# Spectrum rows of an S4 convolution kernel: real and imaginary parts interleaved over the partitions, in place of one half of the partitions each

## The chip, the cores and the metric

The kernel runs on one core of one Trainium2 chip. The metric is the device time of one execution in microseconds (us); the time of the kernel before is the median of three runs. The profile comes from one more execution, with a trace of every engine: PE (TensorE), DVE (VectorE), ACT (ScalarE), POOL (GpSimd) and SP (SyncE, whose queue issues most transfers).

## What is computed

Four residual layers over x of 2048 positions by 512 channels: attention over a dilated window (A), a state-space convolution (B), A again, B again, with a layer norm in front of each.

```python
x = x + A(layernorm(x));  x = x + B(layernorm(x))
x = x + A(layernorm(x));  x = x + B(layernorm(x))

# B: a convolution along the sequence, one kernel K per channel
P  = exp(logdA[:, :, None] * l)
K  = einsum("dn,dnl,dn->dl", Cc, P, dB).real
Kf = rfft(pad(K));  Uf = rfft(pad(u))
y  = irfft(Uf * Kf)[:L] + u * Dskip
```

Both B layers have the same parameters, so the spectrum Kf of the convolution kernel is the same in both.

## The kernel before, in words

`k_gen` makes K in the first 150 us or so, while `build_b_consts` makes the tables of the transform (F1, w2, Wp, WpJ, g2) and layer A's projections run beside it. Then comes A's core, then B (class `FftB`), then A and B again. A's core shifts its values along the partitions by transfers from `v_ext` to itself, partitions 0 to 111 to 1 to 112 in one of them (L305, around 439 us in the second A layer).

B's transform has two steps each way. The 512 channels are cut into 2 groups g (`NG`) of 64 columns of 4 channels (`DQG`). `f1` is the first forward step: 8 tiles per group, each of 16 matmuls (L523) into one PSUM tile `pb`, copied out to `a1s` (L512). `f2` is the second: 8 chunks `ec` of 16 frequencies, each of 16 matmuls against the table `w2_sb` (L532). The rows of its product, which are the 128 partitions, are 64 real rows and 64 imaginary rows of the spectrum: `w2` is built so that rows 0 to 63 are real and rows 64 to 127 imaginary. `i1` and `i2` are the two inverse steps; `i1` contracts over those 128 rows with the tables Wp and WpJ (L574, L575).

The spectrum of K goes through memory, since both B layers use it. `k_f2` copies each chunk from PSUM into a tile `kf_sb` (L512, three buffers) and stores it to `kf_dram[g, ec]`, whose layout is 64 rows of (real, imaginary), by two transfers: partitions 0 to 63 to the real places, 64 to 127 to the imaginary ones (L541, 128 KB each). `u_f2` needs each row of the spectrum of K, real and imaginary, on both partitions that hold this row of u's spectrum. So per chunk two transfers load all 64 rows of 4 KB, once into partitions 0 to 63 and once into 64 to 127 of a slot of `kf_ring` (L556, 256 KB each; 4 slots). ACT copies u's chunk to `ub` (L558, three buffers), and two multiplications on DVE (L559 by the real, L560 by the imaginary part) give `t1` and `t2`, from which `i1` goes on.

The generators are interleaved by `zip_run`: `f1` of group 1 beside `k_f2` of group 0, `f1` of u beside `k_f2` of group 1, `f1` of u's group 1 beside `u_f2` of group 0, then `u_f2` of group 1 beside `i1` of group 0. Copies out of PSUM alternate between ACT and DVE (`evac`), `pb` has four buffers. In the first B layer (time 280 to 357) both the stores and the loads of the spectrum run; `kf_ring` lies there in the memory of `k_perm`, so its first load has to wait for the last matmul that reads `k_perm` (L523 of `f1` of group 1). In the second B layer (540 to 575) only the loads run, and the first four slots are filled some 40 us ahead, in layer A. A scheduler of the build sets the order of instructions on each engine; each engine and the SP queue take theirs in that order.

Of the kernel before, what the change touches and what calls it, by code (L numbers as in the profile page):

```python
# [10 lines left out]
ACT = mybir.ActivationFunctionType  # L11
ALU = mybir.AluOpType
# [3 lines left out]
BF16 = mybir.dt.bfloat16  # L16
I32 = mybir.dt.int32

P = 128
# [345 lines left out]
def build_b_consts(nc, cpool, tmp, w2_dram, g2_dram):  # L365
    C = {}
    pi_i = tmp.tile([P, 1], I32, name="p_i")
# [4 lines left out]
    t_i = tmp.tile([P, 8], I32, name="pk_t")  # L372
    nc.vector.tensor_scalar(t_i[:, 0:1], pi_i[:], 63, 2, ALU.bitwise_and, ALU.logical_shift_right)
    nc.vector.tensor_scalar(t_i[:, 1:2], pi_i[:], 6, None, ALU.logical_shift_right)
    nc.vector.tensor_scalar(t_i[:, 2:3], pi_i[:], 3, None, ALU.bitwise_and)
    nc.vector.tensor_scalar(t_i[:, 3:4], pi_i[:], 15, None, ALU.bitwise_and)
    nc.vector.tensor_scalar(t_i[:, 4:5], pi_i[:], 6, None, ALU.logical_shift_right)
    nc.vector.tensor_scalar(t_i[:, 5:6], pi_i[:], 4, 3, ALU.logical_shift_right, ALU.bitwise_and)
    nc.vector.tensor_scalar(t_i[:, 6:7], pi_i[:], 63, 1, ALU.bitwise_and, ALU.logical_shift_left)
    nc.vector.tensor_copy(t_i[:, 7:8], pi_i[:])  # L380
    pk = tmp.tile([P, 8], F32, name="pk"); nc.vector.tensor_copy(pk[:], t_i[:])
    ak, rik, d4k, cm, rim, d4m = (pk[:, j:j + 1] for j in range(6))
# [5 lines left out]
    dmask_k = tmp.tile([P, 4], F32, name="dmask_k")  # L388
# [4 lines left out]
    def off_cols(name, rcol, v00, v10, v01, v11):  # L393
        o = tmp.tile([P, 2], F32, name=name)
        nc.vector.tensor_scalar(o[:, 0:1], rcol, float(v10 - v00), float(v00), ALU.mult, ALU.add)
        nc.vector.tensor_scalar(o[:, 1:2], rcol, float(v11 - v01), float(v01), ALU.mult, ALU.add)
        return o
# [9 lines left out]
    off = off_cols("w2_off", rik, 2048, 0, 4096, 2048)  # L407
    s8 = 2.0 * math.pi / 8192 * SIN_SHRINK
    ECH = 16
    for ch in range(P // ECH):  # L410
        es = slice(ch * ECH, (ch + 1) * ECH)
        base = tmp.tile([P, ECH, 16], I32, name="w2_base")
        nc.gpsimd.iota(base[:], pattern=[[2, ECH], [512, 16]], base=1 + 2 * ch * ECH, channel_multiplier=0)
        qi = tmp.tile([P, ECH, 2, 16], I32, name="w2_qi")
        for r in range(2):
            nc.scalar.activation(qi[:, :, r, :], base[:], ACT.Identity, scale=ak, bias=off[:, r:r + 1])
        yield
        nc.vector.tensor_scalar(qi[:], qi[:], 8191, None, ALU.bitwise_and)
        sc = tmp.tile([P, ECH, 2, 16], BF16, name="w2_sc")
        nc.scalar.activation(sc[:], qi[:], ACT.Sin, bias=s8 * 4096, scale=-s8)  # L420
        w2f = tmp.tile([P, ECH, 2, 4, 16], BF16, name="w2_full")
        for j in range(4):
            if j < 3:
                nc.scalar.activation(w2f[:, :, :, j, :], sc[:], ACT.Copy, scale=dmask_k[:, j:j + 1])
            else:
                nc.vector.tensor_scalar(w2f[:, :, :, j, :], sc[:], dmask_k[:, j:j + 1], None, ALU.mult)
        (nc.sync if ch % 2 == 0 else nc.scalar).dma_start(w2_dram[:, es, :], w2f[:].rearrange("p e r j m -> p e (r j m)"))
        yield
    yield
    for name, offs in (("Wp", (4, 8, 0, 4)), ("WpJ", (8, 12, 4, 8))):  # L430
# [41 lines left out]
class FftB:  # L472
# [63 lines left out]
    def k_f2(self, g):  # L536
        def consume(p2, ec):
            kf = self.wk.tile([P, DQG, EC], BF16, name="kf_sb")
            self.evac(kf[:], p2[:].rearrange("p e q -> p q e"))
            for ri in range(2):  # L540
                self.nc.sync.dma_start(self.kf_dram[g, ec, :, ri], kf[ri * 64:(ri + 1) * 64])  # L541
        yield from self.f2(g, "ka", consume)

    def u_f2(self, g):
        nc = self.nc
        if self.kf_ring is None:
            self.kf_ring = self.ring_pool.tile([P, 4, 2, DQG, EC], BF16, name="kf_ring", tag="kp")
        t1 = self.gtile("t1", [P, DQG, P])
        t2 = self.gtile("t2", [P, DQG, P])
        self.S[g]["t"] = (t1, t2)  # L550

        def consume(p2, ec):
            kc = self.kf_ring[:, self.nkf % 4]
            self.nkf += 1
            for h in range(2):
                nc.sync.dma_start(self.kf_ring[h * 64:(h + 1) * 64, (self.nkf - 1) % 4], self.kf_dram[g, ec])  # L556
            ub = self.wk.tile([P, DQG, EC], BF16, name="ub")
            nc.scalar.copy(ub[:], p2[:].rearrange("p e q -> p q e"))  # L558
            nc.vector.tensor_tensor(t1[:, :, ec * EC:(ec + 1) * EC], ub[:], kc[:, 0], ALU.mult)  # L559
            nc.vector.tensor_tensor(t2[:, :, ec * EC:(ec + 1) * EC], ub[:], kc[:, 1], ALU.mult)  # L560
        yield from self.f2(g, "ua", consume)
# [247 lines left out]
def kernel(  # L809
# [58 lines left out]
    def after_setup():  # L868
        b_steps(4)
        front0(0)  # L870

    cb["gen"] = build_b_consts(nc, cpool, btmp, w2_dram, g2_dram)
    k_gen(tc, nc, consts["ident"], ins, kd, after_load=la.front_open, after_setup=after_setup, per_chunk=chunk_done)
    b_steps(100)
# [96 lines left out]
```

## Time and profile before

| what | us |
|---|---|
| median of three runs (601.05 to 602.58) | 602.39 |
| the profiled execution, device time | 601.58 |
| its span in the trace | 599.8 |
| DVE busy | 475.8 (79%) |
| PE busy | 373.9 (62%) |
| ACT busy | 356.8 (59%) |
| copies and waits from the first store of the spectrum to the last product, first B layer | 285.7 to 356.5 |
| the products of the second B layer | 540.3 to 575.0 |

A profile's page has, in this order, the busy time of each engine, the span in 40 slices, the DMA queues, the chain of work that ended last, the costliest groups of instructions and the DMA issues. The chain names at each moment what the end was waiting for; a transfer stands in it from its issue to its landing. The table by windows gives, for a stretch of time, the busy time of each engine, the clock granted to PE (1.00 is 2.4 GHz, 0.50 is 1.2 GHz), the mean busy share of the 16 DMA engines and the rate at which they moved bytes.

### The profile page before, as it was taken

Reading aid. Unit: us, or ns where it says so; the run is one execution under the profiler, and the core shown is the slowest. Engines: PE = TensorE matmul, PEld = TensorE weight load, DVE = VectorE, ACT = ScalarE, POOL = GpSimd, SP = SyncE. Lnnn points to the kernel's source line nnn. Section 1 sums busy time; section 2 is a strip of 40 time slices with the busy share of each in tenths; the row PEclk is TensorE's granted clock in tenths of the full one; section 3 lists DMA queues with packets and bytes.
Section 4 is the critical chain, followed back from the end, with each engine's and each line's share of the span. In section 5 each row is a group of like instructions: output and inputs, shape, how many; then the busy total and the mean of one; then the engine's idle time right before and its main releaser. Section 6 shows DMA issues by size and latency. Waiting matters only on the chain.

```text
span 599.8 us, 11233 instructions
## 1 busy us (share of the span) xinstructions
PE 373.9 (62%) x4496; PEld 242.2 (40%) x4536; DVE 475.8 (79%) x828; ACT 356.8 (59%) x603; POOL 44.8 (7%) x47
## 2 busy tenths in 40 slices
PE   1000415643897797586873558499998877764864
PEld 1000103431554353234763557244644432364763
DVE  3789999999496899895674667867989998767665
ACT  3999889878764354667663532694543544667520
POOL 1001020100410000200000000510000011100000
PEclk9999858757899898999996688799998987979878
DMA  6000212111259200208579951200220041268813
GB/s 201 1 1 35 105 70 72 54 56 37 69 176 278 63 1 1 71 1 348 126 161 227 229 147 36 70 1 2 62 61 1 2 108 33 74 278 186 203 37 140
DMA packets 32551, 57.33 MB, mean 96 GB/s; under 512 B 12153, under 2 KB 21498, under 8 KB 30706
## 3 DMA queue, kind: packets, MB, share of 16 engines
q1 hardware_dynamic: 29618, 49.80, 30.2%
q0 software_dynamic: 576, 4.19, 2.0%
q10 hardware_dynamic: 2304, 2.62, 1.3%
q8 instruction: 35, 0.57, 0.4%
q14 instruction: 18, 0.15, 0.1%
HBM read 38.67 MB, written 12.19 MB: 85 GB/s over the span
## 4 chain that ended last, share of the span: by engine, by line
DVE 34%; PE 26%; DMA 12%; ACT 11%; issue 9%; SPq 3%; POOL 3%; DVEq 0%; POOLq 0%; ACTq 0%; another core or an unknown queue 0%
DMA kf_ring<-kf_dram 5%; DVE pav L264 5%; PE po L268 4%; PE pq L299 4%; DVE prod L223 3%; POOL ln_rstd L94 3%; PE pq L201 3%; PE pb L523 2%; DMA v_ext<-v_ext 2%; PE pq L284 2%; DVE cm_a L628 2%; PE L L226 2%; PE pp L154 2%; DMA kf_dram<-kf_sb 2%; DVE x_sb L72 2%
## 5 line engine op out<-in xcount | busy, mean ns | idle before, releaser
L223 DVE TENSOR_TENSOR prod<-qT,kT_ext 128x2048 bf16<-128x2048 bf16 x64 | 75.6, 1215 | 9.7 <-ACT qT L203 9.7
L268 PE MATMUL po<-pav,ident 128*128 128x512 bf16 x245 | 69.2, 402 | 19.7 <-DVE pav L264 18.0
L264 DVE TENSOR_TENSOR pav<-attn,v_ext 128x2048 bf16<-128x2048 bf16 x64 | 76.1, 1214 | 2.9 <-DMA k_rl<-kd_dram 2.5
L574 PE MATMUL pb<-Wp,t 128*128 128x128 bf16 x256 | 39.1, 246 | 26.5 <-DVE t L559 23.6
L558 ACT CAST ub<-pb 128x1024 bf16<-128x1024 f32 x32 | 32.3, 1022 | 24.1 <-DVE t L560 23.7
L268 PEld LDWEIGHTS <-ident 128*128 128x128 bf16 x256 | 25.8, 103 | 51.1 <-issue 30.6
L76 ACT ACTIVATE ln_junk<-x_sb 128x512 bf16<-128x512 f32 x48 | 30.2, 630 | 26.9 <-DVE x_sb L72 26.7
L94 POOL TENSOR_TENSOR ln_rstd<-ln_veps,ln_mh 128x4 f32<-128x4 f32 x16 | 23.1, 1444 | 307.8 <-DVE ln_nm L87 154.7
L148 PE MATMUL pt<-ident,xn 128*128 128x128 bf16 x128 | 12.9, 255 | 51.3 <-DVE xn L104 49.6
L226 PEld LDWEIGHTS <-prod 128*128 128x128 bf16 x1024 | 32.8, 96 | 21.8 <-DVE prod L223 12.2
L271 ACT CAST o_sb<-po 128x512 bf16<-128x512 f32 x32 | 18.5, 581 | 37.7 <-PE po L268 37.6
L284 PE MATMUL pq<-wop,oT 128*128 128x512 bf16 x121 | 34.5, 403 | 9.1 <-ACT oT L281 8.5
L532 PE MATMUL pb<-a1s,w_sb 128*128 128x64 bf16 x768 | 32.3, 199 | 12.3 <-ACT ub L558 8.2
L226 PE MATMUL L<-ind,prod 128*128 128x8 bf16 x1024 | 35.0, 167 | 6.4 <-DVE prod L223 6.2
L574 PEld LDWEIGHTS <-t 128*128 128x128 bf16 x256 | 28.4, 112 | 24.3 <-DVE t L559 24.2
L575 PE MATMUL pb<-WpJ,t 128*128 128x128 bf16 x256 | 38.1, 246 | 0.0
L154 PE MATMUL pp<-xnT,wqk 128*128 128x512 bf16 x122 | 32.7, 401 | 7.9 <-ACT xnT L150 4.4
L512 ACT CAST a1s<-pb 128x1024 bf16<-128x1024 f32 x30 | 29.9, 1017 | 12.6 <-PE pb L523 11.6
L762 PE MATMUL pk<-B_r,A_r 128*128 128x84 bf16 x128 | 18.1, 263 | 30.8 <-DVE A_r L630 30.7
L532 PEld LDWEIGHTS <-w_sb 128*128 128x128 bf16 x768 | 28.4, 102 | 15.3 <-issue 11.6
L559 DVE TENSOR_TENSOR t<-ub,kf_ring 128x1024 bf16<-128x1024 bf16 x32 | 22.0, 686 | 14.6 <-DMA kf_ring<-kf_dram 14.6
L201 PE MATMUL pq<-xnT,wqk 128*128 128x512 bf16 x121 | 31.9, 386 | 2.5 <-ACT qT L203 1.3
(203 smaller groups left out, 995.8 us busy)
## 6 DMA issues: line engine op xcount, KB each, us to landing
kf_ring<-kf_dram SPq DMA_DIRECT2D x64, 256.0 KB, 7.2
w_sb<-w_dram SPq DMA_DIRECT2D x8, 1024.0 KB, 4.9
x_sb<-in_A_x_dram POOLq DMA_DIRECT2D x4, 1024.0 KB, 10.6
kf_dram<-kf_sb SPq DMA_DIRECT2D x32, 128.0 KB, 3.4
v_ext<-v_ext SPq DMA_DIRECT2D x6, 448.0 KB, 4.2
wqk<-in_A_wqkv_dram SPq DMA_DIRECT2D x4, 512.0 KB
xin<-in_A_x_dram SPq DMA_DIRECT2D x4, 512.0 KB, 6.5
w_dram<-w_full SPq DMA_DIRECT2D x4, 512.0 KB, 2.6
```

The source lines that it names most:

```text
L94: nc.gpsimd.tensor_tensor(rstd[:], veps[:], lnst["mh"][:, 0:n], ALU.pow)
L154: nc.tensor.matmul(pp[:], lhsT=self.wqk[:, dt, D + ft * P: D + (ft + 1) * P], rhs=self.xnT[:, dt, b * 512:(b + 1) * 512], start=(dt == 0), ...
L201: nc.tensor.matmul(pq[:], lhsT=wqk[:, dt, ft * P:(ft + 1) * P], rhs=xnT[:, dt, q * 512:(q + 1) * 512], start=(dt == 0), stop=(dt == NDT - 1))
L223: nc.vector.tensor_tensor(pr[:], qT[:, ft].unsqueeze(1).to_broadcast([P, NW, 4, P]), kap, ALU.mult)
L226: nc.tensor.matmul(L[:, al, w0 + wi, ft * 8:(ft + 1) * 8], lhsT=pr[:, wi, al, :], rhs=ind8[:], start=False, stop=True, skip_group_check=True)
L264: nc.vector.tensor_tensor(pv[:], attn[:, al, wg * NW:(wg + 1) * NW, :].unsqueeze(2).to_broadcast([P, NW, DH, H]), vap, ALU.mult)
L268: nc.tensor.matmul(po[:], lhsT=ident[:], rhs=pv[:, wi].rearrange("p d h -> p (d h)"), start=(w == 0), stop=(w == W - 1))
L284: nc.tensor.matmul(pw[:], lhsT=oT[:, ftp, :], rhs=wo[:, ftp, :], start=(ftp == 0), stop=(ftp == NDT - 1))
L532: nc.tensor.matmul(p2[:, j, :], lhsT=self.w2[:, ec * EC + j, :], rhs=a1s[:, ec * EC + j, :], start=True, stop=True)
L558: nc.scalar.copy(ub[:], p2[:].rearrange("p e q -> p q e"))
L574: nc.tensor.matmul(p3[:, j, :], lhsT=t1[:, dql, :], rhs=wp_r, start=True, stop=False)
L575: nc.tensor.matmul(p3[:, j, :], lhsT=t2[:, dql, :], rhs=wpj_r, start=False, stop=True)
```

## The change

The rows of the spectrum are put on the partitions in another order: row r has its real part on partition 2r and its imaginary part on partition 2r + 1. For that, three index columns (`pk_t`) that Wp and WpJ are built from get other shifts and masks, and the table `w2` is written with the real and imaginary column side by side instead of 64 apart: in `build_b_consts` the tiles `w2_qi`, `w2_sc` and `w2_full` have the pair as their last dimension, so that L416 writes every second element, and L424 and L426 write 16 runs of 32 elements where they wrote 32 runs of 16. The count of instructions there is the same.

With that, a chunk of `kf_sb` has the order of `kf_dram` and is stored by one transfer of 128 partitions by 2 KB (16 stores instead of 32). The two loads of a chunk stay two loads of 64 rows by 4 KB, but go to the even and to the odd partitions (`h::2`) instead of to the lower and the upper half. The bytes are the same in all of them. From line 541 on, the line numbers after the change are smaller by one.

```diff
-    nc.vector.tensor_scalar(t_i[:, 3:4], pi_i[:], 15, None, ALU.bitwise_and)
-    nc.vector.tensor_scalar(t_i[:, 4:5], pi_i[:], 6, None, ALU.logical_shift_right)
-    nc.vector.tensor_scalar(t_i[:, 5:6], pi_i[:], 4, 3, ALU.logical_shift_right, ALU.bitwise_and)
+    nc.vector.tensor_scalar(t_i[:, 3:4], pi_i[:], 31, 1, ALU.bitwise_and, ALU.logical_shift_right)
+    nc.vector.tensor_scalar(t_i[:, 4:5], pi_i[:], 1, None, ALU.bitwise_and)
+    nc.vector.tensor_scalar(t_i[:, 5:6], pi_i[:], 5, None, ALU.logical_shift_right)
...
-        qi = tmp.tile([P, ECH, 2, 16], I32, name="w2_qi")
+        qi = tmp.tile([P, ECH, 16, 2], I32, name="w2_qi")
         for r in range(2):
-            nc.scalar.activation(qi[:, :, r, :], base[:], ACT.Identity, scale=ak, bias=off[:, r:r + 1])
+            nc.scalar.activation(qi[:, :, :, r], base[:], ACT.Identity, scale=ak, bias=off[:, r:r + 1])
...
-                nc.scalar.activation(w2f[:, :, :, j, :], sc[:], ACT.Copy, scale=dmask_k[:, j:j + 1])
+                nc.scalar.activation(w2f[:, :, j], sc[:], ACT.Copy, scale=dmask_k[:, j:j + 1])
...
-            for ri in range(2):
-                self.nc.sync.dma_start(self.kf_dram[g, ec, :, ri], kf[ri * 64:(ri + 1) * 64])
+            self.nc.sync.dma_start(self.kf_dram[g, ec].rearrange("p r q e -> (p r) (q e)"), kf[:].rearrange("p q e -> p (q e)"))
...
-                nc.sync.dma_start(self.kf_ring[h * 64:(h + 1) * 64, (self.nkf - 1) % 4], self.kf_dram[g, ec])
+                nc.sync.dma_start(self.kf_ring[h::2, (self.nkf - 1) % 4], self.kf_dram[g, ec])
```

The scheduler orders two queues differently as a result. First the SP queue in the first B layer, from the loads of the tables `w2_sb` and `g2_sb` to the load of layer A's weights. Before:

```order
L493 DMA w_sb<-w_dram 128x4096 x4
L494 DMA g_sb<-g_dram 128x4096
L541 DMA kf_dram<-kf_sb 64x1024 x32
L556 DMA kf_ring<-kf_dram 64x2048 x32
L128 DMA wqk<-in_A_wqkv_dram 128x4x512
```

and now:

```order
L540 DMA kf_dram<-kf_sb 128x1024 x4
L555 DMA kf_ring<-kf_dram 64x2048
L540 DMA kf_dram<-kf_sb 128x1024 x3
L555 DMA kf_ring<-kf_dram 64x2048 x2
L540 DMA kf_dram<-kf_sb 128x1024 x3
L555 DMA kf_ring<-kf_dram 64x2048
L540 DMA kf_dram<-kf_sb 128x1024
L555 DMA kf_ring<-kf_dram 64x2048
L540 DMA kf_dram<-kf_sb 128x1024 x3
L555 DMA kf_ring<-kf_dram 64x2048
L540 DMA kf_dram<-kf_sb 128x1024 x2
L555 DMA kf_ring<-kf_dram 64x2048 x26
```

Six loads, which are three of the four slots of the ring, now stand between the stores; the first of them stands behind the fourth store. In the second B layer the SP queue is as it was.

Then DVE, where the copies of the spectrum of K (`kf_sb`) give way to the products `t` of the first B layer. Before:

```order
L512 CAST kf_sb<-pb 128x1024 x7
L512 CAST a1s<-pb 128x128x8
L512 CAST kf_sb<-pb 128x1024
L512 CAST a1s<-pb 128x128x8 x3
L559 TENSOR_TENSOR t_3829<-ub,kf_ring 128x64x16
L560 TENSOR_TENSOR t_3830<-ub,kf_ring 128x64x16
```

and now:

```order
L512 CAST kf_sb<-pb 128x1024
L512 CAST a1s<-pb 128x128x8
L558 TENSOR_TENSOR t_3813<-ub,kf_ring 128x64x16
L559 TENSOR_TENSOR t_3814<-ub,kf_ring 128x64x16
L558 TENSOR_TENSOR t_3813<-ub,kf_ring 128x64x16
L559 TENSOR_TENSOR t_3814<-ub,kf_ring 128x64x16
L558 TENSOR_TENSOR t_3813<-ub,kf_ring 128x64x16
L559 TENSOR_TENSOR t_3814<-ub,kf_ring 128x64x16
L512 CAST a1s<-pb 128x128x8
L558 TENSOR_TENSOR t_3813<-ub,kf_ring 128x64x16
L559 TENSOR_TENSOR t_3814<-ub,kf_ring 128x64x16
L512 CAST a1s<-pb 128x128x8
```

Two of the three copies `a1s` have moved behind the third and the fourth pair of products. The order on PE in these stages is unchanged.

## Rows read from the trace of the kernel before

**Rows 1.** Chain of waits by line: 278 to 378, then 526 to 600.

```profile
by line: issue 24.1%; DMA kf_ring<-kf_dram 19.4%; DMA kf_dram<-kf_sb 11.3%; PE pb L523 5.5%; SPq L556 5.5%; SPq L541 4.9%; DVE kf_sb L512 4.8%; DVE t L559 4.1%; DVE t L560 3.6%; PE pb L532 3.6%; PE pb L574 2.6%; PE pb L575 2.6%; POOL ln_rst
...
by line: DMA kf_ring<-kf_dram 16.1%; PE pb L523 10.6%; PE pb L574 10.3%; PE pb L575 10.1%; DVE t L559 8.7%; DVE t L560 6.5%; issue 4.8%; DVE xo L591 4.7%; PE pb L588 3.3%; PE pb L532 3.3%; PE pb L589 3.0%; DVE a1s L512 2.2%; DVE z L512 1.7%
```

**Rows 2.** Windows: length, PE, PEld, DVE, ACT, POOL busy, PE clock, DMA share, GB/s.

```profile
280.00:282.00 2.00, 0.87 (x32) 0.86 (x32) 1.94 (x2) 2.00 (x4) 0.00 (x0) 1.00 1.04 422
302.00:304.00 2.00, 2.00 (x61) 1.71 (x57) 1.26 (x2) 1.75 (x2) 0.00 (x0) 1.00 0.90 198
330.00:332.00 2.00, 0.54 (x11) 0.37 (x8) 1.01 (x3) 1.01 (x1) 0.00 (x0) 0.50 1.03 227
439.00:440.00 1.00, 1.00 (x6) 0.39 (x4) 1.00 (x1) 0.76 (x1) 0.00 (x0) 1.00 0.93 242
594.00:596.00 2.00, 0.00 (x0) 0.00 (x0) 0.79 (x1) 0.00 (x0) 0.00 (x0) 1.00 1.01 399
```

**Rows 3.** DVE's timeline, first B layer: start, length, what, [idle before <-ended by].

```profile
285.66 3.48 DVE L512 CAST kf_sb<-pb 128x1024 bf16<-128x1024 f32 x3
...
310.88 1.22 DVE L512 CAST kf_sb<-pb 128x1024 bf16<-128x1024 f32 x1
...
320.19 0.69 DVE L559 TENSOR_TENSOR t<-ub,kf_ring 128x1024 bf16<-128x1024 bf16 x1 [2.57 <-DMA kf_ring<-kf_dram]
...
322.48 0.69 DVE L559 TENSOR_TENSOR t<-ub,kf_ring 128x1024 bf16<-128x1024 bf16 x1 [1.00 <-DMA kf_ring<-kf_dram]
...
355.84 0.68 DVE L560 TENSOR_TENSOR t<-ub,kf_ring 128x1024 bf16<-128x1024 bf16 x1
```

**Rows 4.** Chain in time: start, length, what (copy, issue, landing).

```profile
292.95 1.24 DVE kf_sb L512
...
295.39 0.54 SPq L541
...
295.98 3.68 DMA kf_dram<-kf_sb
```

**Rows 5.** The page's DMA issues: KB each and median us from issue to landing.

```profile
w_dram<-w_full SPq DMA_DIRECT2D x4, 512.0 KB, 2.6
...
g_dram<-g_s SPq DMA_DIRECT2D x8, 128.0 KB, 1.9
```

**Rows 6.** Chain in time: PE's pace at 2.4 and at 1.2 GHz.

```profile
311.65 0.57 PE pb L532 x16
312.23 0.57 PE pb L523 x16
...
338.06 0.11 PE pb L574
```

**Rows 7.** Second B layer: DVE's timeline, then SP's.

```profile
540.34 0.68 DVE L559 TENSOR_TENSOR t<-ub,kf_ring 128x1024 bf16<-128x1024 bf16 x1
...
541.54 0.68 DVE L559 TENSOR_TENSOR t<-ub,kf_ring 128x1024 bf16<-128x1024 bf16 x1
...
574.27 0.68 DVE L560 TENSOR_TENSOR t<-ub,kf_ring 128x1024 bf16<-128x1024 bf16 x1
...
541.65 28.29 SPq L556 DMA_DIRECT2D kf_ring<-kf_dram  x24
```

**Rows 8.** DVE's groups by line, 312 to 357: busy, mean ns, idle before.

```profile
L559 DVE TENSOR_TENSOR t<-ub,kf_ring 128x1024 bf16<-128x1024 bf16 x16 | 11.0, 688 | 10.5 <-DMA kf_ring<-kf_dram 10.5
...
L512 DVE CAST xnT<-pb 128x1024 bf16<-128x1024 f32 x4 | 4.9, 1224 | 3.5 <-PE pb L575 3.5
```

**Rows 9.** ACT's groups by line, 0 to 160 us.

```profile
L416 ACT ACTIVATE w_qi<-w_base,w_off,pk 128x256 int32<-128x256 int32 x16 | 9.1, 593 | 0.0
...
L420 ACT ACTIVATE w_sc<-w_qi 128x512 bf16<-128x512 int32 x8 | 5.0, 630 | 4.0 <-DVE w_qi L418 4.0
...
L725 ACT CAST B_r<-sq_r 128x512 bf16<-128x512 f32 x6 | 3.6, 606 | 0.0
L721 ACT CAST pow_r<-sq_r 128x512 bf16<-128x512 f32 x5 | 3.0, 605 | 0.0
```

More of the change, by code (lines that the diff above doesn't have):

```diff
@@ L413, in build_b_consts @@
         nc.gpsimd.iota(base[:], pattern=[[2, ECH], [512, 16]], base=1 + 2 * ch * ECH, channel_multiplier=0)
-        qi = tmp.tile([P, ECH, 2, 16], I32, name="w2_qi")
+        qi = tmp.tile([P, ECH, 16, 2], I32, name="w2_qi")
         for r in range(2):
-            nc.scalar.activation(qi[:, :, r, :], base[:], ACT.Identity, scale=ak, bias=off[:, r:r + 1])
+            nc.scalar.activation(qi[:, :, :, r], base[:], ACT.Identity, scale=ak, bias=off[:, r:r + 1])
         yield
         nc.vector.tensor_scalar(qi[:], qi[:], 8191, None, ALU.bitwise_and)
-        sc = tmp.tile([P, ECH, 2, 16], BF16, name="w2_sc")
+        sc = tmp.tile([P, ECH, 16, 2], BF16, name="w2_sc")
         nc.scalar.activation(sc[:], qi[:], ACT.Sin, bias=s8 * 4096, scale=-s8)
-        w2f = tmp.tile([P, ECH, 2, 4, 16], BF16, name="w2_full")
+        w2f = tmp.tile([P, ECH, 4, 16, 2], BF16, name="w2_full")
         for j in range(4):
             if j < 3:
-                nc.scalar.activation(w2f[:, :, :, j, :], sc[:], ACT.Copy, scale=dmask_k[:, j:j + 1])
+                nc.scalar.activation(w2f[:, :, j], sc[:], ACT.Copy, scale=dmask_k[:, j:j + 1])
             else:
-                nc.vector.tensor_scalar(w2f[:, :, :, j, :], sc[:], dmask_k[:, j:j + 1], None, ALU.mult)
-        (nc.sync if ch % 2 == 0 else nc.scalar).dma_start(w2_dram[:, es, :], w2f[:].rearrange("p e r j m -> p e (r j m)"))
+                nc.vector.tensor_scalar(w2f[:, :, j], sc[:], dmask_k[:, j:j + 1], None, ALU.mult)
+        (nc.sync if ch % 2 == 0 else nc.scalar).dma_start(w2_dram[:, es, :], w2f[:].rearrange("p e j m r -> p e (j m r)"))
         yield
```

## The prediction

> **What bounds the kernel now.** I read the chain of waits first, by line, over the two B layers. In 278 to 378 us transfers of the spectrum hold 30.7% of it, loads 19.4 and stores 11.3, and in 526 to 600 us the loads hold 16.1% [rows 1]: no engine leads there, the transfers do. Why they are slow is in the table by windows [rows 2]. The load of the tables w2 and g2, 128 partitions, ran at 422 GB/s with the 16 DMA engines full (280 to 282). The ring's loads have the engines just as full, at 227 GB/s (330 to 332). The stores of the last result, 128 partitions, ran at 399 GB/s (594), those of the spectrum at 198 with a share of 0.90 (302). So a transfer into or out of 64 neighbouring partitions keeps all DMA engines busy at about half the rate. Then DVE's timeline shows who waits: the products t follow each other every 2.29 us (320.19 to 322.48) with a wait of 1.00 for the ring each time [rows 3]. A slot is 524,288 bytes, in 2.29 us 229 GB/s, the rate of the windows. In the store stage a copy kf_sb waits for an earlier store to free one of three buffers [rows 4].
>
> The time is made against the profiled execution, 601.6 us; the median of the runs is 0.8 above it, which I add at the end.
>
> **Term 1, the stores of the first B layer.** From the first copy kf_sb to the sixteenth it is 310.88 - 285.66 = 25.2 us, 15 steps of 1.68 [rows 3]. A buffer's cycle now is its copy, two issues, and a landing of 3.68 us [rows 4], since two half-rate stores lie ahead of it. After it is one copy 1.24, one issue 0.54, one landing, and some 0.1 to hand over, for three steps. The landing of a 256 KB store from 128 partitions is in no row; a 128 KB one took 1.9, a 512 KB one 2.6 [rows 5]. I take 2.25, the middle, since the size is between them: 4.1 us, 1.38 a step. That is above what PE asks for, 0.57 for 16 matmuls of f1 and 0.57 of f2 per step [rows 6]. 15 x (1.68 - 1.38) = 4.5. One copy a1s of 1.2 on DVE, which today falls into a wait, eats part of it: 3.3 saved. With 1.9 it is 1.26 a step and 5.1, with 2.6 it is 1.49 and 1.6.
>
> The queue has a new wait: the first load stands behind the fourth store and waits for PE's last read of k_perm, and all later stores stand behind it on SP. PE needs one or two steps more (1.1 to 2.3 us) for that read; the fifth store is late by that once, under three buffers. I count 0 to 1 us, inside the bounds of term 1.
>
> [...]
>
> **Term 2, from the last copy kf_sb to the last product of the first B layer.** 310.88 to 356.52 is 45.6 us [rows 3]. DVE's own work in it: sixteen pairs of products, which follow each other at 1.20 a pair where nothing is waited for (540.34 to 541.54 [rows 7]), 19.2; the copy kf_sb, three a1s and four xnT, eight that take 1.13 each where they stand back to back (three in 3.48, the last with its tail [rows 3]), 9.1. That is 28.3. DVE waits 10.5 for the ring and 3.5 for PE before xnT [rows 8], the rest before the copies a1s. Also the loads stand behind the last store today, and the first product waits for them until 320.19 [rows 3]. After, three slots are loaded between the stores, so the first product follows its ub at once, and two a1s go behind the fourth product at the latest, as work DVE has to do anyway. If the loads keep up, DVE is next, with some 2 us of its wait for PE left: 30.3, and 15.3 saved.
>
> Do they keep up? Thirteen slots remain, from about 311 to the start of the last product at 340; less 2 for a landing that is 27 us, 2.1 a slot, or 250 GB/s on average. But the ring is a loop: slot n + 4 is loaded only when product n is done, and two issues (0.54 each, as the store's [rows 4]), transfer and landing stand in it, so that the rate still counts above 250. At 422 GB/s a slot takes 1.24 us, and I lose nothing; at 300 it takes 1.75, about the mean 1.77 that DVE needs for a pair and half a copy, and I put the loss at 1.5; at 250 at 4; at 229 at 7, which leaves 8, most of it the early first slots.
>
> **Term 3, the second B layer.** 540.34 to 574.95 is 34.6 us [rows 7]. Work: 19.2 for the pairs, six copies 6.8, together 26.0; again 2 for PE: 28, 6.6 saved. Twelve slots are loaded from 541.65 on [rows 7]. They must land by 567 here, so 23 us, 1.95 a slot, 270 GB/s. At 422 nothing is lost, at 300 about 0.5, at 250 4, at 229 all.
>
> **Which rate.** Upper bound 422, the row of the same queue with 128 partitions. Lower, of transfers that lie over nearly all partitions, the copy v_ext of 112 partitions: 242 at a share of 0.93 [rows 2]. [...] I take the middle, about 330, where the loss is 1 and 0.5. A load below 227 has no row that speaks for it, but none that excludes it.
>
> [...]
>
> **The tables.** L416 now writes every second element. L725, which writes 4 of 84 elements, takes 606 ns, and L721, which writes all, 605 [rows 9]: 0. Bound: if the 256 elements cost as 512, by L420 against L416 37 ns each, 16 of them 0.6 us of ACT, in a stage where ACT is nearly full; a gain I exclude, since nothing is removed. Longer runs in L424 and L426: nothing. The new index columns are the same three instructions. The number of loads and matmuls is unchanged; 16 issues fewer on SP, counted in term 1.
>
> **Sum.** 3.3 + (15.3 - 1) + (6.6 - 0.5) = 23.7. 601.6 - 23.7 = 577.9, with 0.8 for the median **578.7**. Nothing behind gives it back: i1 of group 1 and layer A start from the last product. Bounds: all at the good ends 5.1 + 15.3 + 6.6 = 27, 575; landing 2.6 and loads at 250: 1.6 + 11.3 + 2.6 = 15.5, 587.
>
> **Rivals.** [...] (b) PE becomes the bound. Beside i1, a step is 16 matmuls L532 and 16 of L574 and L575. At 1.2 GHz these are 0.11 each [rows 6], 1.7 and about 1.0 for L532, 2.7 where DVE needs 1.77. The clock was 0.50 in 330 to 332, where PE stood for the ring [rows 2]. If it stays there for the 8 steps of both layers: 2 x 8 x 0.93 = 15, of which today's first two steps of each layer, also slow, are 4: 11 lost, 590. Against: PE has more to do per us than before, and fewer stalls. (c) Slower: loads to every second partition are slower than to neighbouring ones. With s us a slot the last product can't start before 311 + 13 s + 2, where it starts at 355.2 today, so term 2 gains 42 - 13 s; term 3 likewise 573.7 - 541.7 - 2 - 12 s = 30 - 12 s; the ring's loop takes some 6 of both, as at 229 GB/s above, and term 1 gives 3.3. Zero is at s = 2.8, about 190 GB/s. At 150 (3.5 us) it is 18 us slower, 620. For it only that no load here has this shape. (d) The new layout doesn't spread the loads at all and the stores gain nothing: only the earlier first slots are left, some 4 us, 598; the rows of 128 partitions speak against it for the stores. (e) Better: loads at 422, and PE's clock stays high as its stalls go, about 2 us a layer less: 571 to 574.
>
> **How the numbers follow.** The forecast (574 to 585) gets 0.57, (a) 0.20, (b) 0.07, (e) 0.10, (c) 0.03, (d) 0.03. The range 573 to 590 leaves out (c), (d), most of (e) and the ends of (a) and (b). This kernel's time can be told from no change beyond about 0.3%, 1.8 us. Slower by that: 0.03, from (c). Within: 0.02, the worse part of (d). Faster: 0.95.
>
> **What would show it.** In the profile after: windows of the first B layer's ring loads with a DMA share near 1 well above 227 GB/s, or a share below 1; stores at 350 or more; the first product of the first B layer within some 2 us of the last copy kf_sb; pairs of products 1.2 to 1.8 us apart instead of 2.29; the wait of L558 for the ring in the first B layer, 10.5 before, under 3. Wrong would make it ring loads still at 227 with a share of 1, PE at 0.50 all through i1, or L416 longer than 0.65 us.

## The result

The changed kernel takes 583.2 us (median of 4 runs, 581.6 to 586.1), the kernel before 602.0 in the same session. The ratio is 0.9695, with a 95% interval of 0.9654 to 0.9736: 18.8 us or 3% faster. The forecast was 578.7 with a range of 573 to 590: the direction and the range hold, the time came out 4.5 us above the forecast. The profiled execution of after took 581.6 us, the fastest of the four; its span is 579.6 against 599.8. (Of the kernel called e8 below, three of six runs lay in a slower state; its row goes by the other three.)

The transfers first: the page's DMA issues of after, with KB each and median us from issue to landing.

```profile
kf_ring<-kf_dram SPq DMA_DIRECT2D x64, 256.0 KB, 4.1
...
kf_dram<-kf_sb SPq DMA_DIRECT2D x16, 256.0 KB, 3.0
```

And windows in which the ring's loads fill the DMA engines, first two of the first B layer, then two of the second (columns as in [rows 2]: the last three are PE's clock, the DMA share, GB/s):

```profile
318.00:320.00 2.00, 1.39 (x48) 1.40 (x48) 2.00 (x4) 0.68 (x2) 0.00 (x0) 1.00 0.98 338
324.00:326.00 2.00, 2.00 (x32) 2.00 (x30) 1.29 (x2) 1.97 (x3) 0.00 (x0) 0.63 0.99 313
...
530.00:532.00 2.00, 0.76 (x26) 0.74 (x26) 2.00 (x4) 1.01 (x2) 0.00 (x0) 1.00 1.02 346
538.00:540.00 2.00, 2.00 (x30) 2.00 (x29) 0.09 (x1) 1.35 (x2) 0.00 (x0) 0.61 1.01 334
```

At the same full share the loads moved 227 GB/s before [rows 2]; now it is 313 to 346. What became of the waits is in DVE's groups by line, in 311 to 343 and then in 523 to 556 (busy, mean ns, idle time before them and what ended it):

```profile
L558 DVE TENSOR_TENSOR t<-ub,kf_ring 128x1024 bf16<-128x1024 bf16 x16 | 11.0, 685 | 0.6 <-DMA kf_ring<-kf_dram 0.5
L512 DVE CAST xnT<-pb 128x1024 bf16<-128x1024 f32 x4 | 4.9, 1224 | 3.9 <-PE pb L574 3.9
...
L558 DVE TENSOR_TENSOR t<-ub,kf_ring 128x1024 bf16<-128x1024 bf16 x16 | 11.0, 684 | 0.6 <-DMA kf_ring<-kf_dram 0.6
L512 DVE CAST xnT<-pb 128x1024 bf16<-128x1024 f32 x4 | 4.9, 1224 | 4.2 <-PE pb L574 4.2
```

The wait of the products for the ring, 10.5 us over the sixteen pairs in [rows 8], is 0.5. The wait of the copies xnT for PE was 3.5 there and is still here, with 3.9: it is now the largest wait of this stretch. DVE's timeline shows where it lies (start, length, what, idle before and its releaser):

```profile
308.87 1.22 DVE L512 CAST kf_sb<-pb 128x1024 bf16<-128x1024 f32 x1
...
311.39 0.68 DVE L558 TENSOR_TENSOR t<-ub,kf_ring 128x1024 bf16<-128x1024 bf16 x1
...
312.59 0.69 DVE L558 TENSOR_TENSOR t<-ub,kf_ring 128x1024 bf16<-128x1024 bf16 x1
...
327.02 1.22 DVE L512 CAST xnT<-pb 128x1024 bf16<-128x1024 f32 x1 [1.66 <-PE pb L574]
328.16 0.68 DVE L558 TENSOR_TENSOR t<-ub,kf_ring 128x1024 bf16<-128x1024 bf16 x1
...
330.23 1.22 DVE L512 CAST xnT<-pb 128x1024 bf16<-128x1024 f32 x1 [0.78 <-PE pb L574]
...
334.09 1.22 DVE L512 CAST xnT<-pb 128x1024 bf16<-128x1024 f32 x1 [1.44 <-PE pb L574]
...
341.81 0.69 DVE L559 TENSOR_TENSOR t<-ub,kf_ring 128x1024 bf16<-128x1024 bf16 x1
```

The first product starts 2.5 us after the last copy kf_sb, not 9.3 us after it as in [rows 3], and pairs follow at 1.20. Then, from 325 on, a copy xnT stands ahead of each of the next four pairs. DVE waits for PE's tile ahead of three of these copies, and the products behind each copy follow it without a wait of their own. The second B layer shows the same:

```profile
524.05 0.68 DVE L558 TENSOR_TENSOR t<-ub,kf_ring 128x1024 bf16<-128x1024 bf16 x1
...
540.33 1.22 DVE L512 CAST xnT<-pb 128x1024 bf16<-128x1024 f32 x1 [2.24 <-PE pb L574]
...
547.15 1.23 DVE L512 CAST xnT<-pb 128x1024 bf16<-128x1024 f32 x1 [1.68 <-PE pb L574]
...
554.87 0.68 DVE L559 TENSOR_TENSOR t<-ub,kf_ring 128x1024 bf16<-128x1024 bf16 x1
```

| stretch, profiled executions | before | after | saved | forecast |
|---|---|---|---|---|
| first to sixteenth copy kf_sb (term 1) | 25.2 | 22.5 | 2.7 | 3.3 |
| last copy kf_sb to last product (term 2) | 45.6 | 33.6 | 12.0 | 14.3 |
| second B layer, products (term 3) | 34.6 | 31.5 | 3.1 | 6.1 |
| everything else | | | 2.4 | 0 |

The stretches are starts of DVE's rows subtracted, with the last product's length added. "Everything else" is what is left of the difference of the spans, 20.2: the start of the copies kf_sb is 0.7 later, the stretch between the two layers' products 2.3 and the tail 0.8 shorter. No term speaks for that, and it is of the size in which runs of one kernel differ.

### The profile page after: what moved, and what is told of

The parts are those of the page before. It is cut to its first block, busy times and chain, and to the rows that moved or that the text cites. A ratio compares the mean times of both kernels' runs of the same rounds, so it can differ in the third digit from the quotient of the medians.

```text
span 579.6 us, 11245 instructions
## 1 busy us (share of the span) xinstructions
PE 374.6 (65%) x4536; PEld 239.4 (41%) x4536; DVE 475.0 (82%) x828; ACT 356.2 (61%) x603; POOL 44.8 (8%) x47
## 4 chain that ended last, share of the span: by engine, by line
DVE 34%; PE 27%; ACT 15%; issue 9%; DMA 9%; POOL 3%; SPq 2%; DVEq 0%; POOLq 0%; ACTq 0%
DVE pav L264 5%; PE po L268 4%; PE pq L299 4%; DVE prod L223 3%; PE pq L201 3%; DMA kf_ring<-kf_dram 3%; POOL ln_rstd L94 2%; PE pb L523 2%; PE pq L284 2%; PE L L226 2%; DVE cm_a L627 2%; DVE x_sb L72 2%; DVE t L558 2%; DMA v_ext<-v_ext 2%; PE pb L573 2%
## 5 line engine op out<-in xcount | busy, mean ns | idle before, releaser
L573 PE MATMUL pb<-Wp,t 128*128 128x128 bf16 x256 | 37.1, 239 | 20.0 <-DVE t L558 17.3
L154 PE MATMUL pp<-xnT,wqk 128*128 128x512 bf16 x128 | 33.6, 405 | 7.4 <-ACT xnT L150 4.3
L761 PE MATMUL pk<-B_r,A_r 128*128 128x84 bf16 x128 | 18.8, 270 | 30.1 <-DVE A_r L629 30.1
L574 PE MATMUL pb<-WpJ,t 128*128 128x128 bf16 x256 | 36.2, 239 | 0.2 <-DVE t L559 0.2
L201 PE MATMUL pq<-xnT,wqk 128*128 128x512 bf16 x128 | 34.7, 406 | 2.1 <-ACT qT L203 1.3
L532 PE MATMUL pb<-a1s,w_sb 128*128 128x64 bf16 x768 | 30.5, 196 | 5.1 <-DVE a1s L512 3.4
L148 PEld LDWEIGHTS <-xn 128*128 128x128 bf16 x128 | 9.6, 115 | 54.6 <-DVE xn L104 51.9
L299 PE MATMUL pq<-wvp,xnT 128*128 128x512 bf16 x128 | 32.1, 378 | 0.0
```

What stands on the lines that cost most here:

```text
L154: nc.tensor.matmul(pp[:], lhsT=self.wqk[:, dt, D + ft * P: D + (ft + 1) * P], rhs=self.xnT[:, dt, b * 512:(b + 1) * 512], start=(dt == 0), ...
L201: nc.tensor.matmul(pq[:], lhsT=wqk[:, dt, ft * P:(ft + 1) * P], rhs=xnT[:, dt, q * 512:(q + 1) * 512], start=(dt == 0), stop=(dt == NDT - 1))
L299: nc.tensor.matmul(pp[:], lhsT=xnT[:, dt, a * P:(a + 1) * P], rhs=wv[:, dt].rearrange("p d h -> p (d h)"), start=(dt == 0), stop=(dt == ND ...
L573: nc.tensor.matmul(p3[:, j, :], lhsT=t1[:, dql, :], rhs=wp_r, start=True, stop=False)
L574: nc.tensor.matmul(p3[:, j, :], lhsT=t2[:, dql, :], rhs=wpj_r, start=False, stop=True)
```

## The experiments

Ratios are taken against runs of the kernel before on the same chip, whose medians were 601.8 to 602.0 us. One thing has to be known of all of them: the build's scheduler orders the queues anew for each kernel, so an edit can move instructions that it doesn't touch. For each kernel it is said which orders it has.

| kernel | us | ratio to before, 95% interval |
|---|---|---|
| before | 602.0 | |
| after | 583.2 | 0.9695 (0.9654 to 0.9736) |
| e1: after, loads to neighbouring partitions | 591.8 | 0.9824 (0.9790 to 0.9858) |
| e2: after, stores in halves (loads behind all stores) | 591.6 | 0.9831 (0.9793 to 0.9868) |
| e7: after, loads behind all stores | 588.9 | 0.9776 (0.9750 to 0.9803) |
| e3: after, one load per slot | 572.1 | 0.9499 (0.9463 to 0.9535) |
| e4: after, four loads per layer only | 564.1 | 0.9371 (0.9345 to 0.9396) |
| e6: after, copies xnT later | 573.4 | 0.9526 (0.9502 to 0.9550) |
| e9: before, copies xnT later | 597.4 | 0.9918 (0.9885 to 0.9951) |
| e8: e3 with five buffers | 568.3 | 0.9442 (0.9407 to 0.9477) |
| e10: e6 with six buffers for kf_sb | 569.6 | 0.9477 (0.9448 to 0.9507) |

**e1, where the loads land.** My theory was that the rate of the loads comes from where they land; the rival that the early slots and the stores carry the gain.

```diff
-                nc.sync.dma_start(self.kf_ring[h::2, (self.nkf - 1) % 4], self.kf_dram[g, ec])
+                nc.sync.dma_start(self.kf_ring[h * 64:(h + 1) * 64, (self.nkf - 1) % 4], self.kf_dram[g, ec])
```

> The changed kernel, with one line back: each load of the ring goes to 64 neighbouring partitions again (h * 64 to h * 64 + 63) instead of to every second one. Stores, tables and orders of the queues stay as changed. The rows then lie on the wrong partitions, so the products multiply the wrong pairs; the work and the bytes are the same. Theory, the rate comes from where the rows land: windows full of ring loads fall from 313-346 GB/s to about 228 at a share of the DMA engines near 1, DVE waits for the ring again in both layers, the second B layer's stretch of products goes from 31.5 back to 34 to 35 us and the first's from 33.6 to 37 to 41 us; 590 to 593 us in all against 583.2. Rival, the gain comes from the earlier first slots and the cheaper stores, and the rate of the loads is not set by where they land: windows above 300 GB/s stay and the time stays within 582 to 585 us.

SP, DVE and ACT have the order of after in these stages, so nothing but the landing place differs. It took 591.8 us, 8.6 more than after. Two windows of e1, one of each layer:

```profile
320.00:322.00 2.00, 0.76 (x26) 0.76 (x27) 2.00 (x4) 1.07 (x2) 0.00 (x0) 1.00 1.06 236
...
542.00:544.00 2.00, 0.00 (x0) 0.00 (x0) 1.29 (x2) 0.00 (x0) 0.00 (x0) 0.76 1.04 234
```

DVE's groups in 313 to 350 and 530 to 566:

```profile
L558 DVE TENSOR_TENSOR t<-ub,kf_ring 128x1024 bf16<-128x1024 bf16 x16 | 11.0, 686 | 4.2 <-DMA kf_ring<-kf_dram 4.0 <-ACT ub L557 0.3
...
L558 DVE TENSOR_TENSOR t<-ub,kf_ring 128x1024 bf16<-128x1024 bf16 x16 | 11.0, 687 | 4.0 <-DMA kf_ring<-kf_dram 4.0
```

The rate falls to 234 to 236 GB/s at a full share, the waits for the ring are back, and the two stretches are 38.6 and 34.6 us: 5.0 and 3.1 more than after. The theory's numbers hold, and the second layer's stretch is that of the kernel before to 0.1 us. The store stretch, too, is longer than in after, 24.2 us against 22.5: six loads run between its stores.

**e2, stores in halves.** The same bytes, two transfers of 64 partitions for each chunk. I meant it to undo the whole stores alone.

```diff
-            self.nc.sync.dma_start(self.kf_dram[g, ec].rearrange("p r q e -> (p r) (q e)"), kf[:].rearrange("p q e -> p (q e)"))
+            for ri in range(2):
+                self.nc.sync.dma_start(self.kf_dram[g, ec].rearrange("p r q e -> (p r) (q e)")[ri * 64:(ri + 1) * 64],
+                                       kf[ri * 64:(ri + 1) * 64].rearrange("p q e -> p (q e)"))
```

> The changed kernel with each store of a chunk of the spectrum cut in two, the lower 64 partitions and the upper 64, 128 KB each, as two issues of SP. Loads, tables and layout stay as changed. Theory, the stores gained because one transfer covers all partitions: the stretch from the first to the sixteenth copy kf_sb goes from 22.5 us back to 24.5 to 25.5, landings near 3.7 us; 585 to 587 us against 583.2. Rival, only the number of transfers in flight and their bytes matter, and two halves in flight together land like one whole: stretch 22.5 to 23.2, 583 to 584 us. A second rival, that the saving in this stretch came from the earlier loads or from the order of DVE's copies, gives 583 as well, but with landings that do get longer.

It took 591.6 us, some 5 more than the theory allowed; the halves land after 3.1 us in the median, where I had expected near 3.7. The cause is in the queues: with 32 stores the scheduler puts all ring loads behind the last store again, as in the kernel before, and the copies a1s ahead of the products. So e2 is another thing than I meant: the kernel before, order of SP and DVE included, with its loads (and what belongs to them) spread. As such it is worth 602.0 - 591.6 = 10.4 us. The store stretch is 25.75 us, against 25.2 before. A window of it, PE's clock, share and rate last:

```profile
304.00:306.00 2.00, 2.00 (x64) 1.76 (x61) 1.26 (x2) 1.73 (x3) 0.00 (x0) 1.00 0.93 204
```

**e7, whole stores, but loads behind them.** To separate what e2 had mixed, I gave after the loads' place of before: the first eight loads are queued behind the last store, by an edge that fixes the order on the queue and waits for nothing.

```diff
+                if self.last_st is not None and self.nkf <= 4:
+                    queue_behind(self.tc, ld, self.last_st)
```

> The changed kernel with all loads of the ring queued on SP behind the sixteenth store, as they stand in the kernel before; stores are whole, loads go to every second partition. Against the kernel with stores in halves (591.6 us, whose queues stand in this same order) it differs by the whole stores alone; against the changed kernel (583.2) by the three early slots alone. Theory, by my terms: whole stores are worth about the 2.7 us measured in the store stretch, the early slots the rest: 588 to 589.5 us, with the first product 7 us or so behind the last copy kf_sb. Rival, the whole stores carry most of the 8.4 us, for instance because the last store lands sooner and everything behind it moves up: 584 to 586 us.

588.9 us, in the theory's range. SP, DVE and ACT now have e2's order but for the place of one copy a1s among the stores. DVE's groups in 286 to 310 (lines are 6 to 8 higher than in after):

```profile
L518 DVE CAST kf_sb<-pb 128x1024 bf16<-128x1024 f32 x14 | 16.5, 1216 | 4.1 <-DMA kf_dram<-kf_sb 2.8 <-PE pb L529 1.3
```

A window with its stores in flight and no load:

```profile
296.00:297.00 1.00, 1.00 (x34) 0.86 (x31) 1.00 (x2) 0.63 (x2) 0.00 (x0) 1.00 1.07 387
```

And its timeline, from the last copy kf_sb to the first product:

```profile
308.73 1.21 DVE L518 CAST kf_sb<-pb 128x1024 bf16<-128x1024 f32 x1
...
313.08 1.23 DVE L518 CAST a1s<-pb 128x1024 bf16<-128x1024 f32 x1 [1.31 <-PE pb L529]
315.50 1.22 DVE L518 CAST a1s<-pb 128x1024 bf16<-128x1024 f32 x1 [1.19 <-PE pb L529]
316.64 0.68 DVE L566 TENSOR_TENSOR t<-ub,kf_ring 128x1024 bf16<-128x1024 bf16 x1
```

Whole stores against halves, e7 against e2: 2.7 us. The two intervals overlap, so the times alone don't show that; the store stretch does, with 22.3 against 25.75, and the rate, 387 GB/s against 204. The issues saved on SP are in it too; no run separates them. The early slots, after against e7: 5.7 us; the first product is 7.9 us behind the last copy kf_sb here and 2.5 in after. It doesn't wait for the ring here: three copies a1s stand ahead of it, as in the kernel before, and wait 3.1 us for PE, where the one that stands ahead of it in after waits 0.2. So a good part of the 5.7 us seems to come from the order: with early slots products can fill DVE's wait for PE. The slots and this order come together, and no run has one without the other. From before to after the three steps are 10.4 (spread loads), 2.7 (whole stores), 5.7 (early slots), together 18.8. In the other order, e1 to after, the spread loads are worth 8.6.

**e3, one load per slot.** One transfer to all 128 partitions, whose source reads each row twice in a row.

```diff
-            for h in range(2):
-                nc.sync.dma_start(self.kf_ring[h::2, (self.nkf - 1) % 4], self.kf_dram[g, ec])
+            src = self.kf_dram[g, ec].rearrange("p r q e -> p (r q e)")
+            src = bass.AP(tensor=src.tensor, offset=src.offset, ap=[list(src.ap[0]), [0, 2], list(src.ap[-1])])
+            nc.sync.dma_start(self.kf_ring[:, (self.nkf - 1) % 4].rearrange("p r q e -> p (r q e)"), src)
```

> The changed kernel with the two loads of a slot made one: one transfer to all 128 partitions, whose source reads every row of the spectrum twice in a row (row 0, 0, 1, 1, ...). Same bytes, half the issues. Theory, the rate goes by how many partitions one transfer covers, and 64 of 128 alternating ones cost something against all 128: windows of ring loads rise from 313-346 toward 400 GB/s. Since DVE waits for the ring only 1.0 us in all after the change, the time falls by no more than about 1 us: 582 to 583.2 us. Rival, the two loads already run on all engines and the rate is set by something that both forms share (rows of 4 KB, reading each row twice): windows stay at 313-346 GB/s and the time at 583. A second rival, one issue less per slot shortens the ring's loop (0.5 us of it is issue) and so lets the loads start earlier: the 0.45 and 0.59 us waits go, with no change of rate.

572.1 us: 11.1 faster than after, where I had expected 1 at most. No theory in the expectation has that. DVE's groups of e3 in 521 to 549.5:

```profile
L559 DVE TENSOR_TENSOR t<-ub,kf_ring 128x1024 bf16<-128x1024 bf16 x16 | 11.0, 688 | 3.0 <-DMA kf_ring<-kf_dram 3.0
...
L512 DVE CAST xnT<-pb 128x1024 bf16<-128x1024 f32 x3 | 3.7, 1220 | 0.2 <-PE pb L575 0.2
```

The wait for the ring has grown, from 0.6 to 3.0. What has gone is the wait of the copies xnT, 4.2 to 0.2, and only two of them lie ahead of the last product instead of four (the window takes in a third that starts behind it). The scheduler had moved them: behind pairs 10, 13, 16 and 16 of the products, where after has them behind 9, 10, 11 and 12. It had also put the last copy a1s of f1 behind the fifth pair instead of the fourth, moved two of ACT's copies ub ahead of its copies xnT, and filled four slots between the stores instead of three.

**e4, hardly any loads.** Left out are all loads but the first four slots of each layer, so twelve of sixteen chunks are multiplied by what lies in the ring.

```diff
-            for h in range(2):
+            for h in range(2 if self.nkf <= 4 else 0):
```

> The changed kernel with only the first four slots of the ring loaded in each layer; the other twelve chunks of each layer are multiplied by what lies in the slots, so the output is not the reference's. It is the floor of the two stretches of products if transfers cost nothing. Theory, after the change the loads hardly hold anything (1.0 us of waits) and what is left is DVE's own work and its wait for PE's tiles of i1: the second layer's stretch goes from 31.5 to 30.5 to 31, the first's from 33.6 to 32.5 to 33.3, the time to 581.5 to 582.5 us. Rival, the wait of DVE's copies for PE's tiles (3.9 and 4.2 us, of which I had kept 2 in each layer) comes from late loads further back in the loop, which hold PE and let its clock fall: the stretches go to 28 to 29 and 30 to 31, the time to 577 to 579 us.

564.1 us, below both ranges. This kernel, too, has the copies xnT later; the groups in 517 to 541.5 show no wait at all before products and copies xnT:

```profile
L558 DVE TENSOR_TENSOR t<-ub,kf_ring 128x1024 bf16<-128x1024 bf16 x16 | 11.0, 688 | 0.0
...
L512 DVE CAST xnT<-pb 128x1024 bf16<-128x1024 f32 x3 | 3.7, 1225 | 0.0
```

Its stretches are 26.4 and 23.9 us. So there were two suspects for the wait of the copies xnT, the transfers and the order, and e3 and e4 had changed both.

**e6, the order alone.** After, both loads as they are, and the four copies xnT of DVE put where e3 has them. The SP queue stays as in after; on ACT one copy ub moves ahead of a copy xnT.

```diff
+            if g == 0 and t % 2 == 1:
+                queue_behind(self.tc, cp, self.last_t[(10, 13, 16, 16)[t // 2] - 1])
```

> The changed kernel with both its loads per slot; only DVE's order is moved: of the four copies xnT that DVE makes beside the products of group 1, the first now stands behind the tenth pair of products, the second behind the thirteenth, the last two behind the sixteenth (after the change they stand behind pairs 9, 10, 11 and 12). This is the order that the kernel with one load per slot (572.1 us) has on DVE. Theory, the waits of these copies for PE (3.9 and 4.2 us) are there because a copy stands ahead of products that are ready: they go, the stretches fall from 33.6 and 31.5 us to 29 to 31 and 27 to 29, and the time to 574 to 577 us; one load in place of two is then worth only the 2 to 5 us that are left. Rival, the order is worth nothing, since the ring's loop of two loads a slot would be waited for in its place: waits for the ring grow by what the others lose, 581 to 584 us, and the 11 us of the kernel with one load are due to the load.

573.4 us: 9.8 of the 11.1 us, just below the theory's range; the stretches, 29.6 and 28.2 us, lie inside theirs. DVE's timeline in the second layer, around the first copy xnT (lines 6 higher):

```profile
537.06 0.69 DVE L564 TENSOR_TENSOR t<-ub,kf_ring 128x1024 bf16<-128x1024 bf16 x1 [0.92 <-DMA kf_ring<-kf_dram]
...
540.21 1.22 DVE L518 CAST xnT<-pb 128x1024 bf16<-128x1024 f32 x1
541.34 0.68 DVE L564 TENSOR_TENSOR t<-ub,kf_ring 128x1024 bf16<-128x1024 bf16 x1
```

The copy comes without a wait. In the two stretches the 8.1 us of waits for PE are gone, waits for the ring rise from 1.0 to 4.6 and for ub from 0 to 2.0, and two copies of 1.13 per layer have moved behind the last product: -8.1 + 3.6 + 2.0 - 4.5 = -7.0, where the stretches together are 7.3 shorter. So the rival came true in part: of the 8.1 us of waits 5.6 come back under other names and 2.5 are gone, and the rest of the gain here, 4.5, are the copies that moved. These cost the tail nothing: it is 22.1 us behind the last product, 24.0 in after. In after DVE waits 3.1 and 3.5 us for PE behind the last products of the two layers, before its first copy z; the moved copies fall into that wait, of which 1.2 and 0 are left. One load in place of two, e3 against e6, makes no difference that the intervals tell, the other moves of e3 included.

**e9, the same order in the kernel before.** Was this a gain that had been open all the time? The edit is e6's, in the kernel before.

> The kernel before, with the one move of DVE's order that took the changed kernel from 583.2 to 573.35 us: the four copies xnT stand behind the tenth, thirteenth and sixteenth pair of products. It waits 3.5 and 3.7 us for PE before these copies. Theory, with half-rate loads the ring is what the products wait for, and this wait lies beside the loads' time: it turns into waits for the ring, whose sum rises from 14.6 toward 18 to 20 us; the time falls by no more than 3 us, 599 to 602. Rival, the order has a price of its own whatever the loads do: the same 8 to 10 us are gained here, 592 to 594 us.

597.4 us: 4.6 gained, between the theory's 3 and the rival's 8 to 10, and nearer the theory. DVE's groups in 312 to 356.5 and 538 to 572:

```profile
L565 DVE TENSOR_TENSOR t<-ub,kf_ring 128x1024 bf16<-128x1024 bf16 x16 | 11.1, 691 | 13.5 <-DMA kf_ring<-kf_dram 13.5
...
L565 DVE TENSOR_TENSOR t<-ub,kf_ring 128x1024 bf16<-128x1024 bf16 x16 | 11.0, 687 | 8.0 <-DMA kf_ring<-kf_dram 8.0
```

The waits for PE, 3.5 and 3.7, are gone, and those for the ring have risen by 3.0 and 4.0, from 10.5 and 4.0: the sum of the waits is the same. What is gained are the copies moved out of the stretches, two of 1.13 in each layer, 4.5 us, which the theory had left out. So with half-rate loads the wait for PE had no price. With faster loads it has one: the same move gains 9.8 us there, 5.2 more than here.

**e8 and e10, more buffers.** In e3 DVE's copies kf_sb wait 5.1 us for stores. e8 is e3 with five buffers for kf_sb and ub; e10 is e6 with a pool of six for kf_sb alone, in the first B layer.

```diff
-        self.wk = self.c_mid.enter_context(tc.tile_pool(name=f"b{t}_wk", bufs=3, reuse_waits="tile"))
+        self.wk = self.c_mid.enter_context(tc.tile_pool(name=f"b{t}_wk", bufs=5, reuse_waits="tile"))
...
+        self.wkf = self.wk if t else self.c_mid.enter_context(tc.tile_pool(name=f"b{t}_wkf", bufs=6, reuse_waits="tile"))
...
-            kf = self.wk.tile([P, DQG, EC], BF16, name="kf_sb")
+            kf = self.wkf.tile([P, DQG, EC], BF16, name="kf_sb")
```

> The kernel with one load per slot (572.1 us), with five buffers in place of three for kf_sb and ub. There DVE's copies kf_sb wait 5.1 us for stores to land (landing 3.6 us, since early loads run beside them). Theory, the buffers take that wait away: the store stretch goes from 24.2 to 19.5 to 21.5 us, the time to 568 to 570 us. Rival, the copies then wait for PE or for SP's queue, where the first early load waits for the last read of k_perm with stores behind it: stretch above 23 us, 571.5 to 572.5 us.

> The changed kernel with the copies xnT later (573.35 us) and six buffers for kf_sb in the first B layer, ub with three as before. Theory, the waits of the copies kf_sb for stores (1.7 to 2.4 us on DVE, and ACT's) go and the store stretch falls from 23.2 to 20 to 21 us: 570.5 to 572 us. Rival, loads and stores share the transfer time, so that what the stores gain the loads lose: first products wait longer, 573 to 574 us.

e8's times scatter from 566.5 to 577.6 us, and the interval of its ratio overlaps e3's, so e8 settles nothing. e10 tells more: 569.6 us, 3.8 less than e6, and 13.6 less than after. The intervals of e10 and e6 just overlap, but every run of e10 (568.6 to 571.6) is below every run of e6 (572.2 to 575.9). Its SP queue has four loads, two slots, between the stores instead of six. DVE's timeline of e10 in the store stretch:

```profile
286.03 8.00 DVE L519 CAST kf_sb<-pb 128x1024 bf16<-128x1024 f32 x7
293.95 1.21 DVE L519 CAST a1s<-pb 128x1024 bf16<-128x1024 f32 x1
295.08 8.00 DVE L519 CAST kf_sb<-pb 128x1024 bf16<-128x1024 f32 x7
```

Fourteen copies without a wait. The last starts at 295.08 + 6 x 1.13 = 301.86, so the stretch is 15.8 us, where theory had 20 to 21. A part is given back behind it: from there to the last product it is 34.2 us, 4.5 more than in e6. That isn't the rival's reason, for the waits for the ring fall, from 2.8 to 1.4; the products wait 2.6 for ub and 0.6 for a copy a1s of ACT, a copy xnT waits 0.8 for PE, and one copy a1s more lies in this stretch. From the first copy kf_sb to the last product it is 50.0 us, against 52.8 in e6, 56.1 in after and 70.9 in the kernel before. It beats both kernels.

## Why the prediction was right, and where it was off

**The mechanism is right.** The spectrum's transfers were the bound, loads of 64 neighbouring partitions move at 227 to 236 GB/s, and spreading them gives 313 to 346 in after: e1 undoes that alone and loses 8.6 us. The time by itself would say little, since the range of 573 to 590 takes in most of rival (a), loads left at 229 to 250 GB/s, as well; the windows and e1 do.

**The rate of the loads is right.** I chose 330 GB/s between 242 and 422; the windows show 313 to 346. That it came out so near is in part luck, for no row of the kernel before had this shape and I took the middle. The loss that I put on it, 1 and 0.5 us, is 0.45 and 0.59 in the waits for the ring.

**Term 1** was 3.3 and measured 2.7. The waits of DVE's copies kf_sb for stores fell from 5.1 to 2.4 us, which is the whole saving; a landing takes 3.0 with loads beside it (2.4 in e7, without them), and I had taken 2.25. With the 3.0, and 0.32 for an issue where I had 0.54, the cycle of a buffer is 4.7 us and a step 1.55; 1.50 was measured. That the stores gain by being whole is shown by e2 and e7: 25.75 and 22.3 us. The sign that I had named, stores at 350 GB/s or more, is there in e7 (387); in after loads run among the stores, and ahead of the first load the DMA share is only 0.55 to 0.59 (288 to 292). The new wait of the queue, 0 to 1 us, doesn't show: stretches of after and of e7, which has no load between its stores, differ by 0.2.

**Terms 2 and 3: one step mis-sized, twice.** The words were "DVE is next, with some 2 us of its wait for PE left" and "again 2 for PE". Of the wait before xnT, 3.5 and 3.7 us in the kernel before, I let nearly half go, with no row that said so. It didn't fall but is 3.9 and 4.2. That is 4.1 of the 5.3 us by which both terms together fall short; the rest are mainly gaps of about 0.1 us between DVE's rows, which I counted at nothing. It takes no faster PE to be rid of the wait: e6 takes it away with the same loads and the same work by putting the copies later in DVE's queue. I should have asked of this wait what I asked of the others: what stands behind the waiting instruction, and was it ready? In the kernel before, the products behind it were not, for their slots were still on the way (e9: the wait only changes its name); once loads are fast, some of them are, and the wait has a price of its own: 2.5 us in the two stretches of e6, and 5.2 by the times, 9.8 less e9's 4.6.

**The early slots** I put at "some 4 us" in rival (d); e7 measures 5.7 for them and the order that comes with them.

**The tables** are as costed: L416 takes 610 ns in after against 593, 0.3 us of ACT over 16 of them, inside the bound of 0.6.

**The rivals.** (a), loads left at 229 to 250 GB/s, was priced at 587 to 591, a saving between the 15.5 of the lower bound and 11.3, term 1's 3.3 with the 8 of term 2 at 229 GB/s; e1 is that case, with 234 to 236 GB/s and 591.8. It was a good price, 0.8 short, for a case that didn't come. (b), PE at the low clock, is there in part: 0.61 and 0.63 in the windows above while the first tiles of i1 run, the waits of 1.66 and 2.24 us ahead of them. But those of 1.68 at 547 and 1.44 at 334 are at the full clock, and e6 has none of them, though PE's clock is 0.50 there too (536 to 538). So (b) isn't needed; whether the two waits would be shorter at the full clock no run shows. The clock's two paces and its fall behind a stall are in the trace of the kernel before. Five matmuls of 512 columns (L154, from 392.77) take 1.24 us at 1.00, the last 0.38 of them, so one starts every 0.215 us, 2.4 columns per ns; those of 128 columns (L574, L575, from 338.07) start every 0.106 us at 0.50, 1.2 columns per ns, and these paces are what [rows 6] gives in GHz. PE's work ends at 350.4 there, and the clock is 1.00 up to 354, 0.71 in 354 to 355 and 0.50 in 355 to 356. (c) and (d) didn't come. (e), loads at 422, would have given at most the 1.0 us of waits for the ring with this order.

**What stays open.** Why a DMA share near 1 gives 313 to 346 GB/s here and 422 in the load of the tables: the placement differs, and so do the length and the repetition of the rows; e3, which reaches all partitions in one transfer, shows 324 and 369 GB/s (below), so reach alone isn't it. And one profiled execution moves by some 2 us where nothing was edited: in e6 the first copy kf_sb starts 2.0 us later than in after. The profiled executions of these two differ by 5.7 us only, the medians by 9.8; what makes up the rest the traces can't show.

## What to carry to other kernels

A wait that lies beside a larger one has no price until the larger one goes (in e9 7.2 us of it went and 7.0 came back as waits for the ring): before crediting a change, list all waits of the waiting engine in that stretch and ask for each whether the instructions queued behind it would be ready afterwards; what would be ready makes it a part of the next bound. Look at the order of the queues of every variant before reading its time as the price of the edit, for an edit of transfers alone can move other instructions as well, as e3's one load did with the copies xnT; here the order alone gives 9.8 of the 11.1 us. And where transfers use a part of the partitions, try spreading their rows over all of them; here that took the loads from 227 to over 313 GB/s.

## What the runs showed of the hardware that I had not expected

The share of busy DMA engines doesn't tell their rate: it is near 1 at 227 to 236 GB/s (64 neighbouring partitions), 313 to 346 (every second partition) and 422 (128 partitions, tables). Within one kind it isn't steady either: of the kernels whose loads are those of after, a window of e2 shows 389 and one of e7 277.

```profile
330.00:332.00 2.00, 0.00 (x0) 0.00 (x0) 1.29 (x2) 1.02 (x2) 0.00 (x0) 0.50 1.04 389
...
332.00:334.00 2.00, 2.00 (x26) 2.00 (x24) 0.17 (x1) 1.51 (x2) 0.00 (x0) 0.50 0.97 277
```

And one transfer of 128 partitions that reads each row twice lies among the same values; two windows of e3:

```profile
322.00:324.00 2.00, 1.03 (x20) 0.87 (x18) 2.00 (x5) 1.60 (x2) 0.00 (x0) 0.50 1.02 324
...
328.00:330.00 2.00, 2.00 (x44) 2.00 (x43) 2.00 (x3) 1.43 (x2) 0.00 (x0) 0.83 1.10 369
```
